# The mirrored half's weights: four gathers on GpSimd's queue replaced by eight copies between SBUF tiles on SyncE's queue

## The chip, the cores and the metric

The kernel runs on one core of a Trainium2 chip. The metric is the device time of one execution in microseconds (us). The core has five engines that run their own instruction streams in order: TensorE (PE in the profile, with its weight loads as PEld), VectorE (DVE), ScalarE (ACT), GpSimd (POOL) and SyncE (SP, which only issues DMAs here). All DMAs, whichever engine issues them, are moved by the same 16 DMA engines. Those that GpSimd issues appear in the profile as the queue "software_dynamic" (q0), those of SyncE and ScalarE as "hardware_dynamic" (q1 and q10).

## The reference

The input x has 8 batches of 3072 rows of 256 columns. Two stages follow each other:

```
X = fft over the 3072 rows, then fft over the 256 columns;  x = real part of X
x_prev = x shifted down by one row (first row zero)
xk = mu_k * x + (1 - mu_k) * x_prev
xr = mu_r * x + (1 - mu_r) * x_prev
k  = max(xk @ w_k, 0)                 # w_k: 256 x 1024
v  = (k * k) @ w_v                    # w_v: 1024 x 256
r  = 1 / (1 + exp(-(xr @ w_r)))       # w_r: 256 x 256
out = r * v
```

## The kernel before

The Fourier part is done as small matrix products on TensorE with tables that are computed on the chip. The real part of such a transform is symmetric, so only half of the rows are transformed. The other, mirrored half is read from the same values with its columns in another order, and so the mixing part needs the rows of w_k and w_r in a second order for the mirrored half. The kernel therefore holds each of these two weights twice: `wk_sb[m][a]` (128 partitions x 1024, 16-bit) and `wr_sb[m][a]` (128 x 256), where m is 0 for the first half and 1 for the mirrored half, and a is the half of the 256 rows of the weight that lies on the 128 partitions. Row p of `w[1][a]` is row p of `w[0][1-a]`, but for p = 0, where it is row 0 of `w[0][a]`.

The weights come from DRAM by indirect DMAs of GpSimd (`gather`, line 142), which take the wanted row of each partition from a column of `row_i` and convert 32-bit to 16-bit numbers on the way. The columns are made by `rows()` with six small iota instructions: columns 0 and 1 serve m = 0, columns 2 and 3 serve m = 1.

The mixing part is cut into 48 chunks: 8 batches, the two halves m, and 3 pieces of 512 rows. Each chunk takes four steps, so the main loop has 192 steps and five more to drain. In each step `k_piece` multiplies by `wk_sb[m]` (line 921) and ScalarE applies the maximum (line 931); VectorE squares (line 941); `v_tile` or, in the first chunks, `v_part` multiplies by w_v (lines 962 and 974); `v_out` multiplies by r on VectorE into one of four buffers `o` (line 984) and SyncE stores the result in two DMAs of 64 partitions each (line 992). `r_item` (line 948) multiplies by `wr_sb[m]`. The Fourier part of the next batches is spread between these steps.

The order of the work is written out by hand: `at(step, f)` puts a piece of work at a step, and at the end `pin_order` fixes the order of the instructions on every engine as written. Chunk 3, batch 0 and m = 1, is the first that uses a mirrored weight; it begins at step 12. The x data come from DRAM on GpSimd's queue too: `load_p` (line 136) and the gathers of `load_m` (line 142) fill one of three `xp` and one of three `xm` buffers per half batch, and `fold` on VectorE (lines 174 and 176) uses them. `loads_0`, `loads_1` and `loads_2` hold the GpSimd work of steps up to 4: the first half's `wr`, batch 1's x data, the mirrored `wk` and `wr`. A small write of VectorE (`load_gate`) holds GpSimd back before loads_0 and loads_1 and at a few later steps.

Of the kernel before, what the change touches and what calls it, by code (L numbers as in the profile page):

```python
# [12 lines left out]
UINT32 = mybir.dt.uint32  # L13
# [7 lines left out]
def _v(ap, extra_offset, free_dims):  # L21
    new_ap = [list(ap.ap[0])] + [[s, c] for (s, c) in free_dims]
    return dataclasses.replace(ap, offset=ap.offset + extra_offset, ap=new_ap)
# [16 lines left out]
def kernel(  # L40
# [10 lines left out]
    nc = tc.nc  # L51
# [3 lines left out]
    P = 128  # L55
# [5 lines left out]
    const = ctx.enter_context(tc.tile_pool(name="const", bufs=1))  # L61
# [16 lines left out]
    def ps_w():  # L78
        return ps_slot("W", 3, 1024)
# [61 lines left out]
    def gather(dst, src, idx):  # L141
        nc.gpsimd.indirect_dma_start(dst, None, src, bass.IndirectOffsetOnAxis(ap=idx, axis=0))  # L142
# [11 lines left out]
    def load_xh(b, h, gs=(0, 1)):  # L154
        if 0 in gs:
            x_tiles(b, h)
        load_p(b, h, 0, gs)
        if h == 0:
            load_m0(b)
        load_m(b, h, 0, 8, idx_g8[:, b, h:h + 1])  # L160
# [57 lines left out]
    wk_sb = [[const.tile([P, F], FP16, name=f"wk{m}{a}") for a in range(2)] for m in range(2)]  # L218
    wr_sb = [[const.tile([P, 256], FP16, name=f"wr{m}{a}") for a in range(2)] for m in range(2)]
# [51 lines left out]
    iota = nc.gpsimd.iota  # L271
    def rows():
        for a in range(2):
            for half in range(2):
                iota(_v(row_i[64 * half:64 * half + 64], a, [(3 - 2 * a, 2)]), pattern=[[0, 2]],
                     base=256 * a + half * (1 - 2 * a), channel_multiplier=2 - 4 * a)
        iota(row_i[0:1, 2:3], pattern=[[0, 1]], base=0, channel_multiplier=0)
        iota(_v(row_i[0:1], 1, [(2, 2)]), pattern=[[0, 2]], base=128, channel_multiplier=0)

    ueo = const.tile([P, 2, 2, 64], INT32)  # L280
    w_eo = const.tile([P, 2, 128], FP16)
    ramp = const.tile([P, P], INT32)
    row_i = const.tile([P, 4], UINT32)
    lo64, hi64 = slice(0, 64), slice(64, 128)

    pcol_i = const.tile([P, 1], INT32)
# [8 lines left out]
    iota(idx_0, pattern=[[S, B]], base=S, channel_multiplier=-32)  # L295
    iota(idx_0[0:1], pattern=[[S, B]], base=0, channel_multiplier=0)
    rows()
    load_m0(0)

# [118 lines left out]
    for c in range(2):  # L418
        nc.scalar.activation(out=tv(TO, 32 * c, (64, 2), (1, 32)),
                             in_=_v(one, 32 * c, [(64, 2), (1, 32)]), func=AF.Copy,  # L420
# [7 lines left out]
    for g in range(2):  # L428
        kw = dict(func=AF.Sin, bias=sc[:, 2 + g:3 + g], scale=sc[:, g:g + 1])
        nc.scalar.activation(out=_v(w_pm, g, [(WA + WB, 2), (2, 2), (4, NU)]),  # L430
                             in_=_v(u_w, 0, [(0, 2), (NU, 2), (1, NU)]), **kw)
        nc.scalar.activation(out=_v(w_pm, WA + g, [(WA + WB, 2), (2, NU)]),
                             in_=_v(u_w, 2 * NU, [(0, 2), (1, NU)]), **kw)
# [27 lines left out]
    def zero_rows():  # L461
        for n in (0, 2):
            nc.gpsimd.memset(xp_sb[n][32:64, 8], 0.0)
# [47 lines left out]
    def loads_1():  # L511
        load_gate()
        load_xh(1, 0, (1,))

    def loads_2():
        for a in range(2):
            gather(wk_sb[1][a], moe_w_k, row_i[:, 2 + a:3 + a])
        load_xh(1, 1)
        for a in range(2):
            gather(wr_sb[1][a], moe_w_r, row_i[:, 2 + a:3 + a])  # L520
        zero_rows()
        quarter_rows()

# [27 lines left out]
    def quarter_rows():  # L551
        iota(same_i, pattern=[[0, 2], [1, 64]], base=0, channel_multiplier=-1)
        nc.gpsimd.tensor_scalar(out=same, in0=same_i, scalar1=0.0, scalar2=None,
                                op0=ALU.is_equal)

    def quarter_tables():
        ps = ps_w()
        nc.tensor.matmul(out=ps[:, 0:128], lhsT=same, rhs=w_eo[:, 1], start=True, stop=True)
        for g, rows in enumerate((lo64, hi64)):
            evac(w_d[rows, 0], _v(w_eo[rows], g, [(2, 64)]), "A")  # L560
            evac(w_d[rows, 1], ps[rows, 64 * g:64 * g + 64], "A")
        for k in range(2):
            nc.gpsimd.memset(_v(w_d[64:65], 64 + k, [(2, 32)]), 2.0 * k - 1.0)
# [473 lines left out]
    w, first = ps_w(), ps_w()  # L1037
# [42 lines left out]
    def at(step, f, *args):  # L1080
        work.setdefault((step, "x" if f in (d_item, d_small, c_item, c_tiles, turned, turned_behind, minus_0, r_item, quarter_tables, a_slot_0) else "w"),
                        []).append((f, args))
# [5 lines left out]
    def event(step, *items):  # L1088
        work.setdefault((step, "e"), []).extend((f[0], f[1:]) for f in items)
# [36 lines left out]
    event(3, (half_tables,))  # L1126
    event(4, (c_item, 0, 25, 2), (c_item, 0, 17, 8))
    at(1, loads_1)
    at(4, loads_2)
    at(8, fold, 1, 0)  # L1130
    at(5, r_item, (0, 0, 0))
# [176 lines left out]
```

## Time and profile before

| what | value |
|---|---|
| median of 3 runs | 426.18 us (425.74 to 427.55) |
| profiled execution, its own time | 426.35 us |
| span of the profiled execution, first to last instruction | 424.6 us |
| TensorE busy | 417.8 us, 98% of the span |
| VectorE busy | 371.0 us, 87% |
| ScalarE busy | 333.3 us, 79% |
| GpSimd busy | 66.4 us, 16% |
| granted TensorE clock | 1.000 |

The profiled execution's time exceeds its span by 1.75 us, which lies before the first and after the last instruction. In the views below, each line of a timeline has the start in us, the length in us, the engine, the line of the kernel, the operation with the tile that it writes and those that it reads, the shapes, the number of instructions merged, and in square brackets how long the engine sat idle before it and on what it waited. Matmuls overlap each other, so a length on PE includes the latency of the last one.

### The profile page before, as it was taken

How to read it: one execution, taken by the hardware profiler on the slowest of the kernel's cores; microseconds unless marked ns; L12 is line 12 of the kernel's file. 1: busy time of each engine (PE TensorE's matmuls, PEld its weight loads, DVE VectorE, ACT ScalarE, POOL GpSimd, SP SyncE). 2: the span in 40 equal slices, each digit the busy share in tenths (PEclk: the TensorE clock that was granted, in tenths of full speed). 3: DMA queues.
4: the chain of work that ended last, by engine and by line, in shares of the span. 5: the costliest groups of instructions: out<-in, count | busy, mean ns of one | idle time of the engine just before them, and what ended most of it. 6: DMA issues, size and time to landing. Idle time of an engine off the chain costs nothing.

```text
span 424.6 us, 9710 instructions
## 1 busy us (share of the span) xinstructions
PE 417.8 (98%) x4004; PEld 293.1 (69%) x4004; DVE 371.0 (87%) x591; ACT 333.3 (79%) x440; POOL 66.4 (16%) x101
## 2 busy tenths in 40 slices
PE   8999999999999999999999999999999999999996
PEld 3767766777667767776767676777777776776765
DVE  8898999999898999989999899989999676977553
ACT  7999886698769986699767996689876897666661
POOL 7488600200060001400041000500000000000000
PEclk9999999999999999999999999999999999999999
DMA  8889972633376233942349232772233232332334
GB/s 170 112 118 218 211 154 57 125 84 66 73 147 151 61 68 54 215 103 51 74 75 225 50 77 56 137 171 58 52 74 77 53 74 51 74 73 54 74 76 99
DMA packets 35217, 42.36 MB, mean 100 GB/s; under 512 B 4147, under 2 KB 31141, under 8 KB 35173
## 3 DMA queue, kind: packets, MB, share of 16 engines
q1 hardware_dynamic: 27488, 25.41, 26.8%
q0 software_dynamic: 7376, 16.08, 22.2%
q8 instruction: 31, 0.51, 0.5%
q10 hardware_dynamic: 308, 0.26, 0.2%
q14 instruction: 14, 0.11, 0.1%
HBM read 32.64 MB, written 25.17 MB: 136 GB/s over the span
## 4 chain that ended last, share of the span: by engine, by line
PE 89%; POOL 5%; DVE 2%; DMA 2%; issue 1%; ACT 0%; POOLq 0%; DVEq 0%
PE psV L962 37%; PE psW L921 35%; PE psW L948 9%; PE psW L598 3%; DMA xm<-in_x_dram,idx_g 2%; POOL xm L142 1%; POOL wr L142 1%; PE psW L237 1%; PE psV L598 1%; POOL xp L136 1%; POOL wk L142 1%; PE psV L380 1%; PE psW L684 1%; PE psW L706 0%; DVE g_all L579 0%
## 5 line engine op out<-in xcount | busy, mean ns | idle before, releaser
L931 ACT ACTIVATE rl<-psW 128x1024 f16<-128x1024 f32 x192 | 194.2, 1039 | 78.8 <-PE psW L921 75.2
L921 PE MATMUL psW<-x,wk 128*128 128x512 f16 (+1 forms) x776 | 194.3, 377 | 0.3 <-DVE x L1058 0.3
L962 PE MATMUL psV<-wv_sb,k 128*128 128x256 f16 x1416 | 183.2, 273 | 0.0
L962 PEld LDWEIGHTS <-k 128*128 128x128 f16 x1424 | 136.7, 98 | 38.6
L941 DVE TENSOR_TENSOR k<-rl 128x2048 f16<-128x2048 f16 (+1 forms) x100 | 115.5, 1157 | 32.8 <-ACT rl L931 32.6
L921 PEld LDWEIGHTS <-wk 128*128 128x128 f16 x776 | 75.5, 98 | 53.9 <-issue 0.6
L984 DVE SCALAR_TENSOR_TENSOR o<-psV,r 128x512 f32<-128x512 f32 x96 | 65.3, 683 | 9.1 <-PE psV L962 8.3
L886 DVE TENSOR_TENSOR x<-y,t 128x1536 f16<-128x1536 f16 (+3 forms) x76 | 62.4, 827 | 2.2
L953 ACT ACTIVATE r<-psW 128x1024 f16<-128x1024 f32 x48 | 49.9, 1040 | 0.8 <-PE psW L948 0.8
L948 PE MATMUL psW<-wr,x 128*128 128x256 f16 x384 | 49.8, 273 | 0.0
L948 PEld LDWEIGHTS <-x 128*128 128x128 f16 x384 | 37.5, 98 | 13.9
L581 ACT ACTIVATE a<-psW 128x832 f16<-128x832 f32 (+4 forms) x36 | 28.7, 848 | 0.7 <-PE psW L650 0.4
L142 POOL DMA_INDIRECT xm<-in_x_dram,idx_g x21 | 27.9, 1331 | 6.4 <-issue 6.4
L581 ACT ACTIVATE g_all<-psW 128x512 f16<-128x512 f32 (+5 forms) x47 | 26.6, 646 | 0.3 <-PE psW L706 0.2
L502 POOL IOTA gate<- 1x1 int32 x7 | 0.9, 126 | 161.3 <-DVE gate L501 161.3
L174 DVE TENSOR_TENSOR p<-xp,xm 112x2304 f16<-112x2304 f16 (+4 forms) x19 | 21.7, 1141 | 0.7 <-DMA xm<-in_x_dram,idx_g 0.7
L875 DVE TENSOR_SCALAR t<-d,muf_t 128x1536 f16<-128x1536 f16 (+3 forms) x43 | 21.9, 518 | 0.1
L581 ACT ACTIVATE pq<-psW 128x1024 f16<-128x1024 f32 (+1 forms) x21 | 20.4, 1006 | 0.1
L875 DVE TENSOR_SCALAR t<-d,mu_m 128x1536 f16<-128x1536 f16 x32 | 19.6, 612 | 0.0
L863 DVE TENSOR_TENSOR d<-y 128x1664 f16<-128x1664 f16 (+5 forms) x19 | 16.7, 880 | 0.4 <-ACT y L581 0.4
L855 DVE TENSOR_TENSOR y<-pq 128x960 f16<-128x960 f16 (+3 forms) x28 | 15.7, 603 | 0.4
L136 POOL DMA_DIRECT2D xp<-in_x_dram x28 | 15.8, 577 | 0.6
(161 smaller groups left out, 233.1 us busy)
## 6 DMA issues: line engine op xcount, KB each, us to landing
out_dram<-o SPq DMA_DIRECT2D x189, 128.0 KB, 2.4
xp<-in_x_dram POOLq DMA_DIRECT2D x13, 216.0 KB, 6.2
xp<-in_x_dram POOLq DMA_DIRECT2D x14, 192.0 KB, 7.1
wv_sb<-in_moe_w_v_dram POOLq DMA_DIRECT2D x1, 512.0 KB, 7.7
xp<-in_x_dram SPq DMA_DIRECT2D x1, 480.0 KB, 4.4
xp<-in_x_dram POOLq DMA_DIRECT2D x1, 384.0 KB, 6.1
xm<-in_x_dram,idx_g POOLq DMA_INDIRECT x21, 7.3
xp<-in_x_dram POOLq DMA_DIRECT2D x1, 288.0 KB, 4.1
```

Source lines behind the costliest of these rows:

```text
L142: nc.gpsimd.indirect_dma_start(dst, None, src, bass.IndirectOffsetOnAxis(ap=idx, axis=0))
L174: V.tensor_tensor(out=p[:, q0:q0 + n], in0=xp[:, q0:q0 + n], in1=_v(xm, o + 256, [(-256, n), (-1, 256)]), op=ALU.add)
L581: nc.scalar.activation(out=out_ap, in_=in_ap, func=AF.Copy)
L875: V.tensor_scalar(out=dst, in0=src, scalar1=mu, scalar2=None, op0=ALU.mult)
L886: V.tensor_tensor(out=_v(x_t[b, j, m], o, [(64 * step, hi - lo), (step, 64)]), in0=y_t[b][:, lo + 3 * m:hi + 3 * m, a], in1=x_t["t", a][:, ...
L921: nc.tensor.matmul(out=st["k", ds][:, 512 * hs + lo:512 * hs + hi], lhsT=wk_sb[m][a][:, 128 * fc:128 * fc + 128], rhs=xk[:, a, 512 * i + l ...
L931: nc.scalar.activation(out=st["rl"][:, 2 * ds:2 * ds + 2], in_=st["k", ds].rearrange("p (f t) -> p f t", f=2), func=AF.Relu, bias=0.0, sca ...
L941: V.tensor_tensor(out=k2_t[c][:, lo:hi], in0=r, in1=r, op=ALU.mult)
L948: nc.tensor.matmul(out=ps[:, 256 * tb:256 * tb + 256], lhsT=x_t[b, 1, m][:, a, 512 * i + 128 * tb: 512 * i + 128 * tb + 128], rhs=wr_sb[m] ...
L953: nc.scalar.activation(out=st["r", c], in_=ps, func=AF.Sigmoid)
L962: nc.tensor.matmul(out=st["v", tb - h][:, 256 * h:256 * h + 256], lhsT=k2_t[c][:, fc, 128 * tb:128 * tb + 128], rhs=wv_sb[:, fc], start=(f ...
L984: V.scalar_tensor_tensor(out=o.rearrange("p a b -> p (a b)")[:, 0:256 * n], in0=st["v", t0][:, 0:256 * n], scalar=16.0, in1=st["r", c][:, ...
```

## The change

The gathers of the four mirrored weight tiles are taken out of `loads_2`, where they stood on GpSimd's queue at step 4. A new function `mirrored_weights`, placed at step 2, issues eight plain DMAs on SyncE's queue from the first half's tiles: for wr and then wk, for a = 0 and a = 1, one DMA copies partitions 1 to 127 of `w[0][1-a]`, and one copies partition 0 of `w[0][a]`. `row_i` loses its two columns for m = 1, and `rows()` writes single columns and needs one iota less.

```diff
     def rows():
         for a in range(2):
             for half in range(2):
-                iota(_v(row_i[64 * half:64 * half + 64], a, [(3 - 2 * a, 2)]), pattern=[[0, 2]],
+                iota(row_i[64 * half:64 * half + 64, a:a + 1], pattern=[[0, 1]],
                      base=256 * a + half * (1 - 2 * a), channel_multiplier=2 - 4 * a)
-        iota(row_i[0:1, 2:3], pattern=[[0, 1]], base=0, channel_multiplier=0)
-        iota(_v(row_i[0:1], 1, [(2, 2)]), pattern=[[0, 2]], base=128, channel_multiplier=0)
+        iota(row_i[0:1, 1:2], pattern=[[0, 1]], base=128, channel_multiplier=0)
...
-    row_i = const.tile([P, 4], UINT32)
+    row_i = const.tile([P, 2], UINT32)
...
+    def mirrored_weights():
+        for w in (wr_sb, wk_sb):
+            for a in range(2):
+                nc.sync.dma_start(out=w[1][a][1:128], in_=w[0][1 - a][1:128])
+                nc.sync.dma_start(out=w[1][a][0:1], in_=w[0][a][0:1])
+
     def loads_2():
-        for a in range(2):
-            gather(wk_sb[1][a], moe_w_k, row_i[:, 2 + a:3 + a])
         load_xh(1, 1)
-        for a in range(2):
-            gather(wr_sb[1][a], moe_w_r, row_i[:, 2 + a:3 + a])
         zero_rows()
         quarter_rows()
...
     at(1, loads_1)
+    at(2, mirrored_weights)
     at(4, loads_2)
```

## The prediction

> **What bounds the kernel now.** I read the busy shares first, then the list of waits.
>
> ```profile
> PE 417.8 (98%) x4004; PEld 293.1 (69%) x4004; DVE 371.0 (87%) x591; ACT 333.3 (79%) x440; POOL 66.4 (16%) x101
> ...
> PE psW L237 <- DVE xm L268: 1.0, 1, 1.0
> ...
> PE psV L974 <- DVE o L984: 0.6, 1, 0.6
> ...
> PE psW L921 <- DVE x L1058: 0.3, 1, 0.3
> ```
>
> TensorE sets the time: its longest waits are 1.0 us at the very start, 0.6 us once at line 974, and 0.3 us once. A change to the loading of weights can therefore win only the 0.6 us or what hangs on it, but it can lose whatever TensorE has to wait. The timeline of TensorE shows where the two touch.
>
> ```profile
> 27.10 1.04 PE L948 MATMUL psW<-wr,x 128*128 128x256 f16 x8
> ...
> 41.07 1.04 PE L921 MATMUL psW<-x,wk 128*128 128x512 f16 x4
> ...
> 50.31 0.60 PE L974 MATMUL psV<-wv_sb,k 128*128 128x256 f16 x4 [0.56 <-DVE o L984]
> ```
>
> The first row is the first use of the first half's wr, at 27.10 us, with no idle time before it: both wr tiles have landed by then. The second row, at 41.07, is step 12 (steps 0 to 11 are the groups of line 921 before it): the first matmuls with `wk_sb[1]`. The third is the 0.56 us stall. It comes from VectorE's queue:
>
> ```profile
> 42.17 1.23 DVE L174 TENSOR_TENSOR p<-xp,xm 112x2048 f16<-112x2048 f16 x1 [0.73 <-DMA xm<-in_x_dram,idx_g]
> ...
> 49.58 1.28 DVE L984 SCALAR_TENSOR_TENSOR o<-psV,r 128x512 f32<-128x512 f32 x2
> ```
>
> The fold of half batch (1,1) waits 0.73 us for its xm gather; from there VectorE has no idle time until the two `v_out` at 49.58, and line 974 waits for the PSUM bank that they read.
>
> **What leaves GpSimd.**
>
> ```profile
> 8.17 0.53 POOL L277 IOTA row_i<- 1x1 uint32 x1
> ...
> 20.11 0.12 POOL L502 IOTA gate<- 1x1 int32 x1 [4.69 <-DVE gate L501]
> ...
> 21.27 1.29 POOL L142 DMA_INDIRECT wr<-in_moe_w_r_dram,row_i  x1 [0.30 <-issue]
> 22.86 1.22 POOL L142 DMA_INDIRECT wr<-in_moe_w_r_dram,row_i  x1 [0.30 <-issue]
> ...
> 28.08 0.95 POOL L142 DMA_INDIRECT wk<-in_moe_w_k_dram,row_i  x1 [0.30 <-issue]
> 29.34 1.74 POOL L142 DMA_INDIRECT wk<-in_moe_w_k_dram,row_i  x1 [0.31 <-issue]
> 31.08 1.20 POOL L136 DMA_DIRECT2D xp<-in_x_dram  x2
> 32.58 2.65 POOL L142 DMA_INDIRECT xm<-in_x_dram,idx_g  x1 [0.30 <-issue]
> 35.54 1.49 POOL L142 DMA_INDIRECT wr<-in_moe_w_r_dram,row_i  x1 [0.31 <-issue]
> 37.33 1.39 POOL L142 DMA_INDIRECT wr<-in_moe_w_r_dram,row_i  x1 [0.30 <-issue]
> ```
>
> The two gathers of wk end 3.0 us after 28.08, so the loads of (1,1), now at 31.08 and 32.58, go out 3.0 us earlier; everything behind the two gathers of wr another 3.2 us. The narrower iotas and the one of 0.53 us that is dropped lie before the 4.69 us that GpSimd waits for its gate: worth nothing, up to 4.69 us. The earlier xm is worth VectorE's 0.73 us and TensorE's 0.56 us; with the small gaps behind it I take -0.7 us, between 0 and -0.8.
>
> **What comes onto SyncE, and by how many DMA engines it is moved.** After an x load at the start, SyncE has nothing to do before its first output:
>
> ```profile
> 31.14 1.41 SPq L992 DMA_DIRECT2D out_dram<-o  x2
> ```
>
> Two issues take 1.41 us there, 0.7 us each. The first copy reads `wr_sb[0][1]` and waits for its landing, by 27.1 at the latest; eight issues are done some 5.6 us later, at 32.7. Behind the waiting copy stand only the outputs from 31.14 on, 1 to 2 us late; for them waits a buffer `o` at its second use. Four exist, and the third pair is due at 49.58, so that delay is covered.
>
> The open quantity is how many of the 16 DMA engines carry a copy of 127 partitions. The trace has no DMA of that shape, but its packet counts tell how others are divided. First the page's row of ScalarE's queue, then its row for the last 5.6 us, with the issues that belong to them:
>
> ```profile
> q10 hardware_dynamic: 308, 0.26, 0.2%
> ```
>
> ```profile
> q10 hardware_dynamic: 304, 0.26, 14.5%
> ...
> out_dram<-o ACTq DMA_DIRECT2D x1, 128.0 KB, 2.9
> ...
> out_dram<-o ACTq DMA_DIRECT2D x2, 64.0 KB, 2.6
> ```
>
> At the end three outputs of 64 partitions send 256 data packets of 1 KB; the other 48 packets are 16 per DMA, one completion from each of 16 engines. The remaining 4 packets of the whole run belong to the two loads of one row of mu: one data and one completion packet each, so one engine each. [...] 64 rows divide evenly into 16 shares, and so do the 96 of the first x load. For 127, a prime, the bounds are one engine (only equal shares) and 16 (shares of 8 with a short last one). Every division seen is into equal shares, and the smallest case did not split its 1 KB further. I take one engine.
>
> [...]
>
> **What one engine needs.** Two copies of wr move 127 x 512 bytes each, two of wk 127 x 2048 bytes: 650 KB, all in one ring, wr first. Three rows price a byte on one engine: SyncE's outputs in 60 to 70 us, ScalarE's row above, and GpSimd's queue in 27 to 60 us (with SyncE's beside it).
>
> ```profile
> q1 hardware_dynamic: 594, 0.54, 26.3%
> ```
>
> ```profile
> q0 software_dynamic: 2147, 4.88, 84.6%
> q1 hardware_dynamic: 1710, 1.56, 14.5%
> ```
>
> Share times 16 engines times the window, divided by the bytes: 42.1 us for 0.54 MB is 78 ns per KB with all engines writing outputs; 13.0 us for 0.26 MB (14.5% of 16 x 5.6 us) is 50; 447 us for 4.88 MB is 92 for loads that convert. So 650 KB take 32.5, 51 or 60 us. I take 32.5, the nearest: for most of the time one engine copies while the others rest, as nearly at the end of the run.
>
> [...]
>
> That engine also carries its sixteenth of GpSimd's loads. From 27 to 60 us these take 84.6% of 33 us, 27.9 us on every engine, less the four gathers (0.66 MB at 92 ns per KB over 16 engines, 3.7 us): 24.2 us. Which goes first matters only if the loads could be put off. A stretch from 47 to 54 us, in which SyncE issued four outputs at 50.29, shows the order:
>
> ```profile
> q0 software_dynamic: 439, 1.48, 105.7%
> q1 hardware_dynamic: 7, 0.01, 0.3%
> ```
>
> ```profile
> 50.29 2.59 SPq L992 DMA_DIRECT2D out_dram<-o  x4
> ```
>
> While GpSimd's queue has a backlog, hardware-queue packets hardly move. So the copies end after loads and copies together: 27.1 + 24.2 + 32.5 = 83.8 us, some 84. The bounds: 27.1 + 32.5 = 59.6 if the copies are served first, and 27.1 + 24.2 + 60 = 111 at the dearest price.
>
> **The sum.** At 41.07 TensorE meets matmuls that need both tiles of `wk_sb[1]`; the last lands at 84. It has no other work in its queue order, so it stands for 43 us, and from there on it is the bound again, so all of it stays. The row-0 copies (5 KB) are in that price. Outputs in the same ring are held until 84 too; the next two need their buffers some 8 us after TensorE resumes, when eight 1 KB packets each for the earlier ones have long gone: nothing. A pause has one more cost. At the start TensorE works at a lower pace for some time:
>
> ```profile
> 6.07 3.35 PE L237 MATMUL psW<-zeros 128*128 128x512 f16 x8
> ...
> 9.93 1.04 PE L237 MATMUL psW<-zeros 128*128 128x512 f16 x4
> ```
>
> The same matmul is 0.39 us apart in the first row and 0.22 in the second (taking off the last one's latency). If it cools in 43 us as before the launch, eight such matmuls cost 8 x 0.17 = 1.4 us. The profiled execution's own 426.35 us + 43 + 1.4 - 0.7 = 470 us; it stands 0.17 us above the median, which I neglect.
>
> **The rivals.** (a) The copies spread over 16 engines and land in time; this is the one that ends on the other side. 650 KB over 16 engines are 2 to 4 us, the last is issued at 32.7, and outputs in the loaded stretch land within 8.8 us of issue at worst:
>
> ```profile
> DMA to landing us min/median/max: 2.4/2.4/8.8
> ```
>
> 32.7 + 8 is just before 41.07. Then only the -0.7 us remains: 425.6. It turns at TensorE's 41.07: each microsecond that a copy lands later costs one. For it: transfers of 64 and 96 rows do use 16 engines. Against it: 127 rows cannot be cut evenly. (b) The same spread, but GpSimd's loads, which go out up to 6 us earlier, form an unbroken backlog and the copies land 2 to 10 us late: 428 to 436. The 0.3% above speaks for it. (c) One engine, but the ring takes turns and SBUF-to-SBUF packets are quick, so that the copies largely pass the loads: landing at 60, TensorE stands 19 us: 444. For it: 1710 packets of SyncE's queue were moved between 27 and 60 us, beside the loads. Against: hardly one in the stretch with a backlog. (d) One engine at the price of the converting loads: landing at 111, 70 us: 497.
>
> **Chances.** One engine 0.90: of it 0.62 near 84 us (455 to 485), 0.14 each for (c) and (d). Sixteen engines 0.10: (a) 0.08, (b) 0.02. The range reaches from (c) to (d), 444 to 497, and leaves out the 0.10 and what lies beyond the bounds. Within 0.5% (2.1 us, about what a measurement of this kernel can tell from no change) lies (a), 0.07, with 0.01 of it for a gain beyond that; TensorE's 98% leaves no room for more. Slower: 0.92.
>
> **What would show it.** TensorE idle before line 921 at about 41 us, waiting for a DMA on SyncE's queue, with the wk copies landing near 84 us. The DMA share near one sixteenth (0.06) once the loads have ended. The packet count of q1: 27488 before; the copies add 512 data packets and, with one engine each, 8 completions (28008), with 16 engines for the four large ones 68 (28068). TensorE's granted clock or its first matmuls after the pause would show the 1.4 us. The fold of (1,1) should not wait any more. No idle time at 41 us and 28068 packets would make this prediction wrong at its main step; idle time that ends at 60 or 110 would make only the price or the order wrong.

## The result and the profile after

The changed kernel takes 463.61 us (median of 6 runs, 463.22 to 465.17), the kernel before 426.09 us in the same comparison. The ratio is 1.0876, with a 95% interval of 1.085 to 1.0902: 37.5 us slower. The forecast was 470 us, with a range of 444 to 497. The profiled execution, from which the views below come, was the longest of the six: 465.17 us, with a span of 463.4 us.

The list of waits of the changed kernel (engine, line, what it waited for: total us, times, longest) names the new wait. Line numbers behind the change are higher by one than before.

```profile
PE psW L922 <- DMA wk<-wk: 35.2, 2, 25.1
...
PE psV L975 <- DVE o L985: 0.8, 1, 0.8
```

TensorE's timeline shows where it lies and how the work goes on behind it.

```profile
32.98 1.20 PE L975 MATMUL psV<-wv_sb,k 128*128 128x256 f16 x8 [0.77 <-DVE o L985]
...
41.93 0.91 PE L666 MATMUL psW<-w_hh,p 48*128 48x104 f16 x32
67.91 0.61 PE L922 MATMUL psW<-x,wk 128*128 128x512 f16 x1 [25.07 <-DMA wk<-wk]
78.61 1.44 PE L922 MATMUL psW<-x,wk 128*128 128x512 f16 x3 [10.09 <-DMA wk<-wk]
79.84 1.92 PE L975 MATMUL psV<-wv_sb,k 128*128 128x256 f16 x8
...
88.48 1.06 PE L707 MATMUL psW<-w_eo,a 128*128 128x128 f16 x16
89.37 0.60 PE L975 MATMUL psV<-wv_sb,k 128*128 128x256 f16 x4
...
96.72 1.89 PE L922 MATMUL psW<-x,wk 128*128 128x512 f16 x8
```

At step 12 TensorE gets one matmul in when `wk_sb[1][0]` has landed, and the other three 10 us later when `wk_sb[1][1]` has. The same places of the kernel before:

```profile
40.23 0.91 PE L665 MATMUL psW<-w_hh,p 48*128 48x104 f16 x32
...
48.69 1.06 PE L706 MATMUL psW<-w_eo,a 128*128 128x128 f16 x16
...
57.93 1.89 PE L921 MATMUL psW<-x,wk 128*128 128x512 f16 x8
```

These rows give a ledger of the 38.8 us between the two spans (463.4 and 424.6). At the second matmul of step 12 the changed kernel is 78.61 - 41.29 = 37.3 us behind (41.29 is 41.07 plus one matmul of 0.22). Of these 37.3 us, 35.2 are the two waits; 1.7 us it was behind already at 41.93 (40.23 before), by stalls such as that at 32.98, and the matmul between the two waits took 0.61 instead of 0.22. The waits end with a landing, so that without the 1.7 us they would only have been longer. At the transforms of line 707 it is 88.48 - 48.69 = 39.8 us behind: 2.5 us more, because the first matmuls after the pause are slow: the three at 78.61 are 0.41 us apart, up to the next row, and those of step 12 before 0.22. At 96.72 it is 38.8 us behind: 1.0 us has come back, since the stall at 50.31 is gone and the small gaps behind it are too. From there to the end nothing changes. So: 37.3 + 2.5 - 1.0 = 38.8.

SyncE's queue (start, length of the issue, what is copied) shows the other half of the story; line 517 is the copy of partitions 1 to 127, line 518 that of partition 0.

```profile
26.49 0.78 SPq L517 DMA_DIRECT2D wr<-wr  x1
27.31 8.69 SPq L518 DMA_DIRECT2D wr<-wr  x1
36.05 1.07 SPq L517 DMA_DIRECT2D wr<-wr  x1
37.16 14.93 SPq L518 DMA_DIRECT2D wr<-wr  x1
52.13 0.61 SPq L517 DMA_DIRECT2D wk<-wk  x1
52.87 5.91 SPq L518 DMA_DIRECT2D wk<-wk  x1
58.82 0.61 SPq L517 DMA_DIRECT2D wk<-wk  x1
59.48 9.76 SPq L518 DMA_DIRECT2D wk<-wk  x1
69.33 39.51 SPq L993 DMA_DIRECT2D out_dram<-o  x18
```

Every issue behind a copy of 127 rows takes 6 to 15 us, and the first output, at 31.14 before, goes out at 69.33.

Three rows by stretch of the span (busy time of PE, PEld, DVE, ACT, POOL, granted clock, DMA share, GB/s) show the machine at rest:

```profile
47.00:52.00 5.00, 0.00 (x0) 0.00 (x0) 0.00 (x0) 0.00 (x0) 0.96 (x2) 0.50 0.98 170
...
57.00:62.00 5.00, 0.00 (x0) 0.00 (x0) 0.00 (x0) 0.00 (x0) 0.00 (x0) 0.50 0.07 25
...
82.00:87.00 5.00, 5.00 (x59) 3.31 (x58) 3.50 (x5) 3.27 (x4) 0.00 (x0) 0.83 0.00 0
```

Until about 52 us the DMA engines are nearly full with loads (0.98 in the first row). Then the DMA share falls to 0.07, one engine of sixteen, which moves 25 GB/s, and no compute engine does anything. The granted clock of TensorE is 0.50 in the pause, against 1.00 in the stretches from 27 to 42 us; a mean of 0.83 from 82 to 87 us, after 0.50 before, puts its return to full speed at about 84 us.

The packet counts of SyncE's queue, before, after, and after from 57 to 67 us (packets, MB, share of 16 engines):

```profile
q1 hardware_dynamic: 27488, 25.41, 26.8%
```

```profile
q1 hardware_dynamic: 28128, 26.06, 25.5%
```

```profile
q1 hardware_dynamic: 149, 0.25, 6.7%
```

SyncE's queue has 640 packets more than before. The four large copies have 508 rows and so, at one packet per row, 508 data packets; from 57 to 67 us 119 of the 149 packets are of 512 B and more and carry the 0.25 MB, 2 KB or one row of wk each. The other 132 are the pieces and completions of the row-0 copies and the completions of the large ones, taken as one from each engine that takes part, since ScalarE's outputs have 16 each. If a row-0 copy goes by n engines, with n pieces and n completions, and a large one by m, then 8n + 4m = 132; with n at most 16 and m dividing 127 evenly, or m = 16, only n = 16 and m = 1 fit. By these counts each copy of 127 rows was moved by one engine. The share from 57 to 67 us, 6.7% or about one sixteenth, says the same.

### The profile page after: what moved, and what is told of

Its sections match the earlier page's. It is cut to its first block, busy times and chain, and to the rows that moved or that the text cites. A ratio compares the mean times of both kernels' runs of the same rounds, so it can differ in the third digit from the quotient of the medians.

```text
span 463.4 us, 9720 instructions
## 1 busy us (share of the span) xinstructions
PE 420.8 (91%) x4004; PEld 293.8 (63%) x4004; DVE 371.7 (80%) x591; ACT 333.2 (72%) x440; POOL 59.1 (13%) x96
## 3 DMA queue, kind: packets, MB, share of 16 engines
q1 hardware_dynamic: 28128, 26.06, 25.5%
## 4 chain that ended last, share of the span: by engine, by line
PE 82%; SPq 7%; issue 6%; DMA 4%; DVE 0%
PE psW L922 34%; PE psV L963 34%; PE psW L949 9%; SPq L518 6%; DMA wk<-wk 4%; PE psW L599 2%; PE psV L975 1%; PE psV L599 1%; SPq L517 1%; PE psW L707 1%; PE psW L651 0%; PE psW L813 0%; PE psW L963 0%; DVE o L985 0%; SPq L246 0%
## 5 line engine op out<-in xcount | busy, mean ns | idle before, releaser
L922 PE MATMUL psW<-x,wk 128*128 128x512 f16 (+1 forms) x776 | 196.2, 379 | 35.5 <-DMA wk<-wk 35.2
L963 PE MATMUL psV<-wv_sb,k 128*128 128x256 f16 x1416 | 183.2, 273 | 0.0
L949 PEld LDWEIGHTS <-x 128*128 128x128 f16 x384 | 37.6, 98 | 14.3 <-issue 0.5
L142 POOL DMA_INDIRECT xm<-in_x_dram,idx_g x21 | 25.6, 1218 | 6.4 <-issue 6.1
L975 PE MATMUL psV<-wv_sb,k 128*128 128x256 f16 x112 | 15.7, 283 | 0.8 <-DVE o L985 0.8
```

Of the source, the lines that this page charges most:

```text
L922: nc.tensor.matmul(out=st["k", ds][:, 512 * hs + lo:512 * hs + hi], lhsT=wk_sb[m][a][:, 128 * fc:128 * fc + 128], rhs=xk[:, a, 512 * i + l ...
L949: nc.tensor.matmul(out=ps[:, 256 * tb:256 * tb + 256], lhsT=x_t[b, 1, m][:, a, 512 * i + 128 * tb: 512 * i + 128 * tb + 128], rhs=wr_sb[m] ...
L963: nc.tensor.matmul(out=st["v", tb - h][:, 256 * h:256 * h + 256], lhsT=k2_t[c][:, fc, 128 * tb:128 * tb + 128], rhs=wv_sb[:, fc], start=(f ...
```

## The experiments

The theory: SyncE's queue divides a DMA into equal shares of rows, so 127 rows go by one engine; that engine has to move all copies beside its part of the loads, and TensorE waits for the last. Its rivals: SyncE's queue position is the trouble whatever the shape; copies between SBUF tiles are slow in themselves; the waits of the row-0 copies or the held outputs cost the time.

### 112 and 15 rows instead of 127

```diff
-                nc.sync.dma_start(out=w[1][a][1:128], in_=w[0][1 - a][1:128])
+                for lo, hi in ((16, 128), (1, 16)):
+                    nc.sync.dma_start(out=w[1][a][lo:hi], in_=w[0][1 - a][lo:hi])
```

> The copy of partitions 1 to 127 is cut into 16 to 127 (112 rows, sixteen equal shares) and 1 to 15 (15 rows, fifteen equal shares); queue, order and waits stay. Theory (127 rows go by one DMA engine): the weights land before TensorE asks for them at some 42 us, TensorE does not stand there, about 426 us, 425.5 to 428. Rival 1 (SyncE's queue is the trouble: the copies or their issues are held behind the loads' backlog, whatever their shape): the 35 us of standing stay for the most part, 445 to 463 us. Rival 2 (a copy from SBUF to SBUF is slow in itself, by bytes): no change, 463 us.

Measured: 428.63 us (8 runs), ratio to the kernel before 1.0056 (1.0038 to 1.0074). Nothing but the cut of one DMA into two was changed, and 35 of the 37.5 us are gone. Rivals 1 and 2 fall with it. It stayed above the theory's upper end by 0.6 us. The profiled execution, at 431.69 us the longest of the eight, shows a small rest of the same wait:

```profile
42.43 0.38 PE L923 MATMUL psW<-x,wk 128*128 128x512 f16 x1 [0.86 <-DMA wk<-wk]
44.69 1.44 PE L923 MATMUL psW<-x,wk 128*128 128x512 f16 x3 [1.89 <-DMA wk<-wk]
```

The likely reason, not tested by itself, is that twelve issues and the order wr before wk put the last wk copy into the loads' backlog, where even sixteen engines deliver it 2.8 us too late; the next kernel, with wk first and eight issues, has no such wait. This is the prediction's rival (b), at the small end of its price.

### All 128 rows, then row 0 over them

```diff
-        for w in (wr_sb, wk_sb):
+        for w in (wk_sb, wr_sb):
             for a in range(2):
-                nc.sync.dma_start(out=w[1][a][1:128], in_=w[0][1 - a][1:128])
-                nc.sync.dma_start(out=w[1][a][0:1], in_=w[0][a][0:1])
+                nc.sync.dma_start(out=w[1][a], in_=w[0][1 - a])
+        for w in (wk_sb, wr_sb):
+            for a in range(2):
+                nc.sync.dma_start(out=w[1][a][0:1], in_=w[0][a][0:1])
```

> Four copies of all 128 partitions first (wk, then wr), then the four copies of row 0 over them, which wait for the landing of the first. Theory (the row count sets the number of engines; 128 is sixteen equal shares): about 426 us, 425.5 to 428, and SyncE's issues take 0.6 to 1 us each, not 6 to 15. Rival 1 (SyncE's queue): 445 to 463 us. Rival 3 (the waits of the row-0 copies hold SyncE's outputs): a stall of TensorE near 50 us, where the third pair of outputs needs a buffer, 428 to 440 us.

Measured: 426.56 us (10 runs), ratio 1.0004 (0.9988 to 1.0019): no difference from the kernel before. One row more per copy, and wk first, and TensorE has no wait for a copy at all. SyncE's issues are short: each of the eight took 0.5 to 1.7 us, and the rest of the lengths below, each over two issues, lies between them.

```profile
26.65 1.11 SPq L517 DMA_DIRECT2D wr<-wr  x2
27.80 2.40 SPq L520 DMA_DIRECT2D wk<-wk  x2
33.74 3.12 SPq L520 DMA_DIRECT2D wr<-wr  x2
```

Rival 3 falls too, as far as the waits of the row-0 copies go; what held outputs can cost is tried below. TensorE's only stall over 0.5 us behind the start is now 0.62 us at 32.15, where VectorE had been held by ScalarE; the one at 50 us is gone. The changed kernel's profile has such a stall at 32.98 (0.77 us), while the last three runs below, with the same compute up to there, have one of 0.4 to 0.5 us near 40 us instead. Such stalls come and go. What the freed GpSimd queue gives is no larger than what such small waits take, and no gain can be measured.

### 122 and 5 rows

```diff
-                nc.sync.dma_start(out=w[1][a][1:128], in_=w[0][1 - a][1:128])
+                for lo, hi in ((1, 123), (123, 128)):
+                    nc.sync.dma_start(out=w[1][a][lo:hi], in_=w[0][1 - a][lo:hi])
```

> The copy is cut into 122 rows (two equal shares of 61) and 5 rows. Theory (one engine per equal share, the largest even number of shares up to 16): each of two engines has half of the 28 us, the last wk copy lands some 14 us earlier than with 127 rows, about 64 us, and the time is about 449 us (446 to 453). A division into sixteen shares with a short last one would give 426 us; a rule that all uneven row counts go by one engine 463 us.

Measured: 450.36 us (one run), as the theory of equal shares has it.

```profile
59.52 0.58 PE L923 MATMUL psW<-x,wk 128*128 128x512 f16 x1 [17.49 <-DMA wk<-wk]
64.55 1.44 PE L923 MATMUL psW<-x,wk 128*128 128x512 f16 x3 [4.44 <-DMA wk<-wk]
```

```profile
q1 hardware_dynamic: 28152, 26.06, 26.4%
```

The last copy lands 14.1 us earlier than with 127 rows. The packets count 664 more than before: 508 rows, 64 pieces and 64 completions of the row-0 copies, and 28 for four pairs of large copies, 7 each, as 2 engines for 122 rows and 5 for 5 would give. The other two kernels add up in the same way: 28248 packets with 112 and 15 rows (31 completions for each pair, 16 + 15 engines), 28192 with 128 (16 each).

### wk before wr

```diff
-        for w in (wr_sb, wk_sb):
+        for w in (wk_sb, wr_sb):
```

> The two wk copies are put before the two wr copies; still 127 rows. Theory (one ring, served in order, with the loads' backlog first): TensorE's first need, both tiles of wk, is met after the loads' share and 254 packets of 83 ns, 27 + 24 + 21 = 72 us, not 78.6: about 457 us. If the ring takes turns with the loads packet by packet, whatever the size, some 230 packets of wk pass during the backlog and it lands near 58 us: 444 us. If SyncE's blocked issues set the time, no change: 463 us.

Measured: 453.46 us (one run), between the two.

```profile
67.83 1.44 PE L922 MATMUL psW<-x,wk 128*128 128x512 f16 x3 [20.78 <-DMA wk<-wk]
```

The theory's 72 was too late. Two things play in, and this run does not part them: the first copies of wk did not have to wait for the wr gathers and were issued some 8 us earlier (the row-0 one at 18.84 instead of 27.31); and the ring took turns with the loads here. Between 30 and 50 us, with only copies on SyncE's queue:

```profile
q0 software_dynamic: 1005, 3.03, 85.8%
q1 hardware_dynamic: 66, 0.13, 2.1%
```

1005 packets of loads are 63 per engine on average; the copies' 66, nearly all of them on their one engine, make it about one for one.

### The same copies on GpSimd's queue

```diff
-                nc.sync.dma_start(out=w[1][a][1:128], in_=w[0][1 - a][1:128])
-                nc.sync.dma_start(out=w[1][a][0:1], in_=w[0][a][0:1])
+                nc.gpsimd.dma_start(out=w[1][a][1:128], in_=w[0][1 - a][1:128])
+                nc.gpsimd.dma_start(out=w[1][a][0:1], in_=w[0][a][0:1])
```

> The eight copies, 127 rows and 1 row as before, are issued on GpSimd's queue instead of SyncE's. If the division of 127 rows is a property of every queue, they go by one engine again and the last wk copy lands between 55 and 80 us: 440 to 465 us. If GpSimd's queue divides otherwise (all its DMAs so far have sixteen completions), the copies land near 40 us; eight issues of 0.6 to 1.2 us put the loads behind them 5 to 7 us later, VectorE's fold of (1,1) then waits a few us: 426 to 430 us.

Measured: 427.22 us (4 runs), ratio 1.0035 (1.001 to 1.006). TensorE never waits for a copy: on GpSimd's queue the wk copies of 127 rows landed 4.3 us after their issue (median). What is lost is GpSimd's time.

```profile
34.08 1.06 POOL L136 DMA_DIRECT2D xp<-in_x_dram  x2
```

```profile
51.47 0.60 PE L975 MATMUL psV<-wv_sb,k 128*128 128x256 f16 x4 [0.94 <-DVE o L985]
```

The loads of (1,1) go out at 34.08, 3.0 us later than before, and the stall of TensorE that hangs on them grows from 0.56 to 0.94 us. The rest of the 1.5 us to the kernel before was not followed.

### Nothing waits for the copies

```diff
-                                 lhsT=wk_sb[m][a][:, 128 * fc:128 * fc + 128],
+                                 lhsT=wk_sb[0][a][:, 128 * fc:128 * fc + 128],
...
-                                 rhs=wr_sb[m][a], start=(a == 0), stop=(a == 1))
+                                 rhs=wr_sb[0][a], start=(a == 0), stop=(a == 1))
```

> All eight copies stay on SyncE's queue, but the mirrored half is multiplied with the first half's weights, so nothing waits for a copy. What is left is what the copies do to others. If TensorE's wait for the weights is all, about 426 us. If SyncE, held in its issues until some 69 us, also holds the outputs, the third pair of outputs (about 50 us) finds no free buffer, VectorE and then TensorE stand until about 72 us: 445 to 450 us.

Measured: 456.63 us (one run), 31 us slower than the kernel before, although no matmul needs a copy.

```profile
PE psV L975 <- DVE o L985: 28.3, 2, 27.8
```

```profile
77.73 1.33 DVE L985 SCALAR_TENSOR_TENSOR o<-psV,r 128x512 f32<-128x512 f32 x2 [27.91 <-DMA out_dram<-o]
```

```profile
58.15 9.75 SPq L518 DMA_DIRECT2D wk<-wk  x1
68.00 12.40 SPq L993 DMA_DIRECT2D out_dram<-o  x11
```

SyncE issues its first output at 68.00, and it lands only at 77.7, when VectorE's third pair of outputs gets its buffer and goes on. These 9.7 us, against a median of 2.4 from issue to landing in the kernel before, are read as the output's share in the same ring, behind the copies. The second expectation had the cause right and the landing 6 us too early, by reckoning from the issue alone. In the changed kernel this second wait lies in the shadow of the first: there VectorE's third pair of outputs comes only at 87.44 us, and finds its buffer free.

### TensorE kept busy in the pause

```diff
     def k_piece(c, ds):
+        if c == chunks[3] and ds == 0:
+            keep_busy(160, ps_w())
```

> 160 matmuls on zeros (some 35 us) are put before the first matmul with a mirrored weight, so that TensorE is busy and not idle while it waits; all else as in the changed kernel. If the pause itself costs TensorE a slower start (2.5 us by the rows behind the pause), the time falls to about 461 us and the granted clock stays at 1.0; if not, 463.6 us.

Measured: 461.55 us (2 runs), 2.1 us less than the changed kernel.

```profile
41.72 34.71 PE L237 MATMUL psW<-zeros 128*128 128x512 f16 x160
...
77.52 0.81 PE L922 MATMUL psW<-x,wk 128*128 128x512 f16 x3 [0.88 <-DMA wk<-wk]
```

The three matmuls behind the wait take 0.81 us, not 1.44, and the mean granted clock over the run is 1.000 instead of 0.959. From these matmuls to the end of the span it is 382.3 us here and 384.8 in the changed kernel: the slower start costs 2.5 us, as in the ledger.

### The loads of batches 2 and 3 held back

```diff
-    at(9, load_xh, 2, 0)
-    at(12, load_xh, 2, 1)
-    at(13, load_xh, 3, 0)
+    at(13, load_gate)
+    at(13, load_xh, 2, 0)
+    at(13, load_xh, 2, 1)
+    at(13, load_xh, 3, 0)
```

> The loads of half batches (2,0), (2,1) and (3,0) are held by a gate until VectorE has passed step 12, so that the copies have the DMA engine for themselves after the loads of batch 1. Theory (loads first, then 28 us of copies on one engine): without some 15 us of the loads the last wk copy lands near 62 to 66 us instead of 78.6, TensorE goes on there, and then stands once more for the late loads at step 16: 450 to 458 us in all. If the copies' own pace sets the landing, it stays near 78 us.

Measured: 450.73 us (one run).

```profile
53.63 0.61 PE L922 MATMUL psW<-x,wk 128*128 128x512 f16 x1 [11.95 <-DMA wk<-wk]
64.34 1.44 PE L922 MATMUL psW<-x,wk 128*128 128x512 f16 x3 [10.10 <-DMA wk<-wk]
```

Without the later loads the last copy lands at 64.3 instead of 78.6 us. From 27 to 60 us GpSimd's queue took 24.3% of 33 us there, 8.0 us on every engine, against 72.1% or 23.8 us in the changed kernel. With 15.8 us of loads less the landing is 14.3 us earlier, so it is about the sum of the engine's part of the loads and of the copies. TensorE did not stand a second time for the late loads, so the time is at the lower end of what was expected.

## Why the prediction was right

**The bound and where it bites: right.** TensorE at step 12 waits for `wk_sb[1]`, and the wait stays in full, because nothing behind it has slack.

**One engine for 127 rows: right, and now shown** by the packet counts and by the four ways of cutting the same rows. The engine counts that follow from the packets are 1 for 127 rows, 2 for 122, 5 for 5, 15 for 15, 16 for 112 and 128. The step that led there had a weak part, however. It took from the loads of mu that a single row stays whole. The single-row copies between SBUF tiles were cut into 16 pieces each, and so the forecast count of 28008 packets was missed (28128). That count cost nothing, but the argument from the smallest case was not sound; that from equal shares held for the six row counts above.

**The landing, 84 us: 78.6.** The term that was mis-sized is the price of the copies, 32.5 us for 650 KB. From 57 to 67 us, alone on its engine, the ring moved 0.25 MB in 6.7% of 16 x 10 us = 10.7 us, 43 ns per KB, which is below all three prices that were weighed (50, 78 and 92). With it the copies take 28 us and the sum is 27.1 + 24.2 + 28 = 79.3. The 10.7 us between the landings of the two wk copies of 260 KB give 41 ns per KB, by a second way. The term of the loads, 24.2 us, was right: from 27 to 60 us GpSimd's queue took 72.1% of 33 us, 23.8 us on every engine. The 25 GB/s measured here on one engine are above the 20 GB/s per engine of ScalarE's outputs (0.26 MB in 13.0 us).

**The order, loads first: wrong in kind, harmless in effect.** The row of 47 to 54 us, in which SyncE's packets hardly moved, covers only the first 3.7 us after the outputs were issued at 50.29. From 54 to 56 us in the same trace, with GpSimd's queue still at 98.4%, 83 of SyncE's packets went beside 201 of its own; why none went sooner stays open. In the run with wk first, whose ring had copies to move from 30 to 50 us, its packets went about one for one with the loads' (66 beside 63 per engine). The end of the last copy does not depend on it, because, as the sum above bears out, the engine is never idle before; rival (c) does not follow from taking turns, since the loads are on the engine all the same.

**The outputs, "nothing": only in this cover.** The prediction held the outputs back until 84 us and let them cost nothing because TensorE stands anyway. That is what happened, and 87.44 is the 8 us behind TensorE's return that it had reckoned with; but with the weights' wait gone they cost 31 us by themselves. What it had not seen at all is SyncE's stretched issues. It had eight issues done by 32.7 us; they were done at 69.

**The gain, -0.7 us, and the slow start, +1.4 us: -1.0 and +2.5.** GpSimd did issue the loads of (1,1) 3.3 us earlier (27.74 instead of 31.08), and the stall at line 974 went. In this kernel that proves little, since the pause gave the loads 37 us more; the run with 128 rows, where the stall went too, is the better sign. The slow start lasted from 78.6 to about 84 us; the prediction had taken the eight slow matmuls of one row of the start for the whole of it.

**The sum.** 37.3 us to the landing, 35.2 of them standing, against 42.7 (83.8 - 41.1) forecast, 2.5 against 1.4, -1.0 against -0.7: 38.8 against 43.4, on 426.35 us.

```profile
27.74 1.16 POOL L136 DMA_DIRECT2D xp<-in_x_dram  x2
```

## What to carry to other kernels

Before a DMA moves to a hardware queue, look at the number of rows that it names: on SyncE's queue here 127 rows went by one engine of sixteen, 122 by two, 112 and 128 by sixteen, and leaving one row out of a full tile put some 28 us of copying on a single engine. The slow copies also held what stood behind them, the first output until 69.33 us instead of 31.14, and in the run where no matmul waited for a copy this cost 31 us by itself; so look at the first wait and at the one in its shadow. And a queue that is freed is worth only what waits for it: here TensorE had 0.6 us to win.

## What the runs showed that was not expected

The issue of a small DMA behind a one-engine copy took 6 to 15 us in the changed kernel, and with wk first one such issue took 33 us:

```profile
25.85 33.05 SPq L518 DMA_DIRECT2D wk<-wk  x1
```

When the one engine had nothing else to do, the issue took 9.8 us, close to the time of the 127 packets ahead of it (260 KB at 43 ns per KB, 11 us). Here SyncE seems to have got rid of its packets only as fast as the ring took them. That reading is inferred from the lengths and was not tested by itself.

By the packet counts the four single-row copies between SBUF tiles went in 16 pieces on 16 engines (64 pieces and 64 completions of the 640 packets more), while the two single-row loads of mu from DRAM went whole on one (4 packets). What decides between them was not tried.

The iotas that fill `row_i` became fewer and narrower, and no time was won. The four of line 275 took 1.22 us together, from 0.65:

```profile
7.45 1.22 POOL L275 IOTA row_i<- 64x1 uint32 x4
...
20.61 0.12 POOL L501 IOTA gate<- 1x1 int32 x1 [4.16 <-DVE gate L500]
```

That is not their form: three of the four took 0.12 to 0.13 us, as before, and one, from 7.98 us on, took 0.69. In the kernel before, the two iotas behind the four took 0.53 and 0.46 us and also ended near 8.7 us. Some delay lies at that place in both kernels; what it is was not tried. It costs nothing here, as GpSimd waits 4.16 us for its gate behind it.
